# A list scheduler whose memory model is told 270 instead of 360 bytes per nanosecond

## The chip, the cores and the metric

The kernel runs on one core of a Trainium2 chip. That core has five engines that work side by side, each through its own list of instructions in a fixed order: TensorE (PE: matrix products, with a part that loads weights, PEld), VectorE (DVE), ScalarE (ACT), GpSimd (POOL) and SyncE (SP), which here does nothing but issue transfers. They meet at semaphores. The metric is the device time of one execution in microseconds (us).

## The reference

Three layers run one after the other on 4 x 576 = 2304 tokens of width 512, all in float32:

```python
# attention: 4 batches, 8 heads, 576 positions, head width 64
scores = scale * np.matmul(q, k.transpose(0, 1, 3, 2))
kth = np.partition(scores, -32, axis=-1)[..., -32:-31]
scores = np.where(scores >= kth, scores, -1000000000.0)
attn = softmax(scores); x = attn @ v
# a small MLP, 512 -> 2048 -> 512 (its weights arrive as float64)
h = x @ w_in
x = (h * np.cos(h)) @ w_out
# eight experts, 512 -> 1024 -> 512, every token through all of them
P = exp(x @ w_gate - max), normalised 8 times by rows and by columns
out = sum(P[:, e] * (np.maximum(x @ w1[e], 0) @ w2[e]) for e in range(8))
```

## The kernel before

Nothing is issued while the program is written down. Every step is put into a plan (`add`, through `put` and `dma`) with its engine, an estimate of its duration in nanoseconds, what it reads and writes, and a priority. At the end `Plan.issue` runs a list scheduler over the plan: it keeps a clock for each engine, takes the engine that can go on first, and there the ready step of the best priority (class of work first, then program order). The order in which it does so is the order in which each engine's instructions are emitted. The chip then runs these lists as they are: an engine whose next instruction waits does not take another one first. So the planner's estimates change no instruction; they change the order.

A step on one engine becomes ready for another after the latency in the table `LAT`. A transfer is a step on SP with a cost of its own; then the planner lets it pass through one shared queue (`dma_free`) at a fixed number of bytes per nanosecond, and its data are ready 900 ns later. The clock of TensorE is modelled as well (the cost doubles when it was not busy enough).

The work, in the order of the time line:

- *Leading tiles.* The first 3 tiles of 128 tokens (tile 0, 1, 2) go alone through attention (`attention_tile`) and the small MLP (`moe1_tile_a`, `moe1_tile_b`) in plain float32, so that expert work for them can begin early. A head's attention: score matmul (L451), copy to SBUF (L457), then on VectorE the search for the 32nd largest of 576 scores: four MAX8 (L459, L465) and three MATCH_REPLACE8 (L464), then the masked exponential (L466) and a reciprocal (L469); GpSimd scales (L468, L470), TensorE transposes (L475) and multiplies with v (L530), ScalarE copies the result into the tile's `x_f` (L534). The MLP multiplies with w_in (L631), forms the gate (L590 to L597), transposes (L640), multiplies with w_out (L656), transposes back (L663) and forms the logits of the gate network (L604, L605). Its weights come through four buffers `wp` of 512 KB.
- *Decode.* Beside that the float64 weights of the small MLP are turned into float32 by DVE, ACT and POOL (L325 to L333) and written back to memory (`win_d`, `wout_d`), from where `wp` reads them.
- *Attention of batch 0 onwards* (`attention`) with the score as a product of split operands (L447, L448) and the product with v at L501 and L503. Its key buffers (`kh`, `kl`, `qs`, made at L345, L347, L430, L431) lie in memory that the decode used before, so it starts after the last decode step.
- *Expert work for the 3 leading tiles* (`fill`, matmuls at L372 to L374): it fills TensorE while VectorE is busy with attention. Its buffers lie where the leading tiles' buffers were, so it starts when all three leading tiles are done.
- The small MLP of the next 512 tokens (`moe1`, 690 to 800 us; L372 to L374, L383, L384, L387), more attention with more expert work for 4 tiles, the MLP for the rest, and from about 1600 us on the experts for the other 15 tiles on TensorE.

TensorE multiplies float32 operands in two ways here: plain (L451, L530, L631, L656: two records in the trace for each matmul) and as products of a high and a low part.

## Time and profile before

| | |
|---|---|
| median of 3 runs | 2468.45 us (2467.83 to 2468.59) |
| the profiled execution | 2470.82 us, span 2469.0 us |
| mean granted TensorE clock | 0.981 |
| busy: TensorE, VectorE, ScalarE, GpSimd | 2367.0, 1988.3, 1279.0, 1282.3 us |
| moved by transfers | 267.44 MB |

The span runs from the first to the last instruction of the profiled execution; what is left of its 2470.82 us lies around it. Times in the rows below count from the span's start. A chain of waits leads back from the last instruction; 58% of it lies on TensorE and 21% on VectorE.

### The profile page before, as it was taken

The page shows a single profiled execution, that of the slowest core. Times are in us where ns is not written, and L with a number is a line of the kernel's source. Part 1 is how long each engine was busy: PE and PEld are TensorE (multiplying, and loading weights), DVE is VectorE, ACT ScalarE, POOL GpSimd, SP SyncE. Part 2 cuts the span into 40 slices and gives each one's busy share as a digit, 9 for nine tenths or more (in the row PEclk, how much of TensorE's full clock was granted, in tenths as well). Part 3 has the DMA queues.
Part 4 walks back from the last instruction along what each step waited for, and adds up shares of the span by engine and source line. Part 5 has one row for each costly group of instructions (what it writes and reads, how often), then busy time and mean ns, then how long its engine had stood idle before and what let it go on. Part 6 is the DMA issues. An engine that isn't in the chain of part 4 may idle for free.

```text
span 2469.0 us, 33830 instructions
## 1 busy us (share of the span) xinstructions
PE 2367.0 (96%) x11161; PEld 1906.4 (77%) x11161; DVE 1988.3 (81%) x3659; ACT 1279.0 (52%) x2470; POOL 1282.3 (52%) x1352
## 2 busy tenths in 40 slices
PE   6888899999988999999999999999999999999999
PEld 3444588888866887888887888788888888888887
DVE  8998599999999999999987787776666666666655
ACT  6785566666787666666666675323222222222221
POOL 6886487778886566666520034433433334443330
PEclk9679999999999999999999999999999999999999
DMA  8766654545522333343343333022222221111101
GB/s 266 225 211 197 192 167 143 159 131 175 172 77 86 115 116 116 119 119 100 91 122 116 97 111 96 26 65 89 78 84 79 73 60 35 39 43 39 35 22 48
DMA packets 162449, 267.44 MB, mean 108 GB/s; under 512 B 15392, under 2 KB 62576, under 8 KB 162272
## 3 DMA queue, kind: packets, MB, share of 16 engines
q1 hardware_dynamic: 162272, 265.27, 35.7%
q8 instruction: 88, 1.44, 0.3%
q14 instruction: 89, 0.73, 0.1%
HBM read 233.34 MB, written 31.87 MB: 107 GB/s over the span
## 4 chain that ended last, share of the span: by engine, by line
PE 58%; DVE 21%; POOL 4%; issue 3%; ACT 2%; DMA 1%; POOLq 0%; SPq 0%; ACTq 0%; DVEq 0%
PE y L372 9%; PE y L373 9%; PE y L374 9%; DVE wk L464 5%; DVE m L465 4%; DVE ex L466 3%; PE g L374 2%; PE g L373 2%; PE g L372 2%; DVE atl L494 1%; PE y L383 1%; PE y L387 1%; DVE m L459 1%; PE y L384 1%; DVE gl L761 1%
## 5 line engine op out<-in xcount | busy, mean ns | idle before, releaser
L347 POOL TENSOR_TENSOR wlo<-raw,whi 128x512 fp32r<-128x512 f32 x336 | 455.8, 1360 | 192.2 <-ACT whi L345 104.1
L465 DVE MAX8 m<-wk 128x8 f32<-128x576 f32 x432 | 318.1, 748 | 1.8
L955 DVE SCALAR_TENSOR_TENSOR acc<-y,P,acc 128x512 f32<-128x512 f32 x308 | 228.7, 747 | 99.6 <-PE y L374 99.3
L345 ACT ACTIVATE whi<-raw 128x512 fp32r<-128x512 f32 x416 | 259.3, 627 | 92.5 <-PE y L374 32.1
L464 DVE MATCH_REPLACE8 wk<-m,wk 128x576 f32<-128x576 f32 x288 | 213.6, 742 | 1.6
L372 PE MATMUL y<-whi,gh 128*128 128x512 f32 x448 | 181.6, 405 | 0.0
L372 PE MATMUL y<-gh,xh 128*128 128x512 f32 x450 | 177.2, 394 | 0.0
L373 PE MATMUL y<-gl,xh 128*128 128x512 f32 x450 | 176.4, 392 | 0.0
L374 PE MATMUL y<-whi,gl 128*128 128x512 f32 x448 | 176.3, 393 | 0.0
L374 PE MATMUL y<-gh,xl 128*128 128x512 f32 x450 | 176.1, 391 | 0.0
L373 PE MATMUL y<-wlo,gh 128*128 128x512 f32 x448 | 175.8, 392 | 0.0
L475 PE MATMUL t<-ident,ex 128*128 128x128 f32 (+1 forms) x720 | 135.6, 288 | 31.3 <-POOL ex L470 6.2
L457 ACT ACTIVATE sc<-s 128x288 f32<-128x288 f32 x288 | 117.2, 407 | 88.8 <-DVE ex L466 46.0
L475 PEld LDWEIGHTS t<-ident,ex 128*128 128x128 f32 (+1 forms) x720 | 86.5, 140 | 94.4 <-POOL ex L470 22.9
L466 DVE SCALAR_TENSOR_TENSOR ex<-sc,m,ex 128x576 f32<-128x576 f32 x144 | 154.6, 1074 | 1.6
L461 ACT ACTIVATE ex<-sc,m 128x576 f32<-128x576 f32 x144 | 111.4, 774 | 38.7 <-POOL m L460 37.2
L470 POOL TENSOR_SCALAR ex<-ex,m 128x576 f32<-128x576 f32 x144 | 112.5, 782 | 33.0 <-DVE m L469 30.4
L493 ACT ACTIVATE ath<-t 64x128 fp32r<-64x128 f32 (+3 forms) x272 | 104.6, 396 | 47.9 <-PE t L475 46.1
L459 DVE MAX8 m<-sc 128x8 f32<-128x576 f32 x144 | 107.0, 744 | 10.0 <-ACT sc L457 9.9
L464 DVE MATCH_REPLACE8 wk<-m,sc 128x576 f32<-128x576 f32 x144 | 106.6, 740 | 0.1
L372 PEld LDWEIGHTS y<-gh,xh 128*128 128x128 f32 x450 | 85.2, 189 | 19.0 <-DVE acc L951 1.0
L372 PE MATMUL y<-gh,gh 128*128 128x512 f32 x254 | 99.4, 391 | 0.0
(376 smaller groups left out, 7093.9 us busy)
## 6 DMA issues: line engine op xcount, KB each, us to landing
raw<-in_w_dram SPq DMA_DIRECT2D x384, 256.0 KB, 2.7
kq<-in_kq_dram SPq DMA_DIRECT2D x40, 576.0 KB, 4.2
raw<-win_d SPq DMA_DIRECT2D x64, 256.0 KB, 3.0
raw<-wout_d SPq DMA_DIRECT2D x64, 256.0 KB, 2.6
y_d<-st SPq DMA_DIRECT2D x56, 256.0 KB, 3.3
raw<-y_d SPq DMA_DIRECT2D x56, 256.0 KB, 2.7
wp<-win_d SPq DMA_DIRECT2D x24, 512.0 KB, 4.8
wp<-wout_d SPq DMA_DIRECT2D x24, 512.0 KB, 4.3
```

The costliest lines, as they stand in the source:

```text
L345: put("ACT", act_ns(n), lambda: A_.activation(hv(), rv(), AF.Copy), [rb], [hb])
L347: put(e, c, lambda: f.tensor_tensor(lv(), rv(), hv().bitcast(F32), op=ALU.subtract), [rb, hb], [lb])
L372: T_.matmul(o(), ah(), bh(), start=start, stop=False)
L373: T_.matmul(o(), ah(), bl(), start=False, stop=False)
L374: T_.matmul(o(), al(), bh(), start=False, stop=stop)
L457: put("ACT", act_ns(288, psum=True), lambda c=c: A_.activation(sc.ap[:, c], o(), AF.Copy), [ps_s], [(sc, c.start, c.stop)])
L459: put("DVE", 669, lambda: V.max(mc(0, 8), sc.ap), [sc], [(m, 0, 8)])
L464: put("DVE", 669, lambda r=r, src=src: V.match_replace(wk.ap, mc(8 * r, 8), src.ap, LOWEST), [src, (m, 8 * r, 8 * r + 8)], [wk])
L465: put("DVE", 669, lambda r=r: V.max(mc(8 * r + 8, 8), wk.ap), [wk], [(m, 8 * r + 8, 8 * r + 16)])
L466: put("DVE", 729, lambda: V.scalar_tensor_tensor(ex.ap, sc.ap, mc(31), ex.ap, op0=ALU.is_ge, op1=ALU.mult, accum_out=mc(33)), [sc, ex, (m, ...
L475: T_.transpose(pt()[:p, c - c0, :], ex.ap[:, c * 128 : c * 128 + p], ident.ap)
L955: put("DVE", 663, lambda y=y, av=av, pcol=pcol: V.scalar_tensor_tensor(av(), y.ap, pcol(), av(), op0=ALU.mult, op1=ALU.add), [y, P, a], [a])
```

## The change

The planner's rate for transfers falls from 360 to 270 bytes per nanosecond. This is the whole diff:

```diff
@@ -197,7 +197,7 @@
                     a = z
             free[e] = op.end = t + cost
             if e == "SP":
-                dma_free = max(t + cost + 650.0, dma_free) + op.bytes / 360.0
+                dma_free = max(t + cost + 650.0, dma_free) + op.bytes / 270.0
                 op.end = dma_free + 900.0
             order.append(k)
             for o in op.outs:
```

Both programs have the same instructions on every engine. Three places show how their order moves. The numbers at the ends of names are buffer numbers, which differ between the two programs.

TensorE at the end of tile 2's attention, in the program of before: from the last L530 of that tile on. `h` and `y` are accumulators, `x_f_277` is tile 2's input to the MLP, `gT` is a gated tile, and L656 with `gT_1242` belongs to tile 1.

```order
L530 MATMUL t<-at_f_304,vp_101 64x128 x5
L447 MATMUL s<-kh_1383,qt_1372 128x288
L448 MATMUL s<-kl_1388,qt_1372 128x288
L447 MATMUL s<-kh_1399,qt_1380 128x288
L448 MATMUL s<-kl_1419,qt_1380 128x288
L631 MATMUL h<-wp_366,x_f_277 128x512
L631 MATMUL y_353<-wp_512,x_f_277 128x512
L631 MATMUL h<-wp_322,x_f_277 128x512 x2
L631 MATMUL y_353<-wp_446,x_f_277 128x512 x2
L631 MATMUL h<-wp_366,x_f_277 128x512 x2
L631 MATMUL y_353<-wp_512,x_f_277 128x512 x2
L656 MATMUL y_1232<-wp_322,gT_1242 128x512 x2
```

The same engine and place in the program of after, from the same L530 on; `gT_814` is the gated tile 0, `x_f_257` tile 2's input.

```order
L530 MATMUL t<-at_f_282,vp_101 64x128 x5
L656 MATMUL y_1246<-wp_368,gT_814 128x512 x2
L656 MATMUL y_1246<-wp_404,gT_814 128x512 x2
L656 MATMUL y_1246<-wp_493,gT_814 128x512 x2
L631 MATMUL h<-wp_368,x_f_257 128x512 x2
L447 MATMUL s<-kh_1427,qs_1435 128x288
L448 MATMUL s<-kl_1437,qs_1435 128x288
L631 MATMUL h<-wp_404,x_f_257 128x512 x2
L447 MATMUL s<-kh_1427,qs_1435 128x288
L448 MATMUL s<-kl_1437,qs_1435 128x288
L656 MATMUL y_1246<-wp_577,gT_814 128x512 x2
L447 MATMUL s<-kh_1442,qs_1445 128x288
```

Tile 0's last eight matmuls at L656 and six of tile 2's at L631, as well as the first score matmuls of the next attention, stood ahead of that L530 and now stand behind it. Counted from it to the first L372, there are 10 of L631 and 32 of L656 before, and 16 and 40 after.

ScalarE at the same time, before: `kh`, `qs`, `qt` and `vs` are the next attention's prepared operands, `x_f_277` is filled by tile 2; the last L534 that fills it stands 28 rows behind the first `kh`.

```order
L461 ACTIVATE ex_223<-sc_213,m_267 128x576
L345 ACTIVATE kh_1383<-kq_117 128x576
L430 ACTIVATE qs_1386<-kq_117 128x128
L430 ACTIVATE qt_1372<-kq_117 128x64
L534 ACTIVATE x_f_277<-t 64x128
L345 ACTIVATE vs_1393<-vraw_120 128x5x64
L345 ACTIVATE kh_1399<-kq_122 128x576
L479 ACTIVATE at_f_304<-t 128x512
```

ScalarE after, where the first L534 shown is tile 2's last:

```order
L479 ACTIVATE at_f_282<-t 64x128
L534 ACTIVATE x_f_257<-t 64x128
L345 ACTIVATE kh_1427<-kq_115 128x576
L430 ACTIVATE qs_1435<-kq_115 128x128
L430 ACTIVATE qt_1429<-kq_115 128x64
L345 ACTIVATE vs_1440<-vraw_119 128x5x64
L345 ACTIVATE kh_1442<-kq_122 128x576
L430 ACTIVATE qs_1445<-kq_122 128x128
```

The preparation stood among tile 2's copies and now stands behind the last of them.

TensorE in the small MLP of the next 512 tokens, before: L383 and L384 multiply a gated tile `gh` with w_out, L447 and L448 here are the second half of one head tile's score matmul.

```order
L383 MATMUL y_353<-gh_2057,whi_1726 128x512
L384 MATMUL y_353<-gh_2057,wlo_1741 128x512
L447 MATMUL s<-kh_1399,qs_1406 128x288
L448 MATMUL s<-kl_1419,qs_1406 128x288
L383 MATMUL y_766<-gh_2057,whi_1726 128x512
L384 MATMUL y_766<-gh_2057,wlo_1741 128x512
```

The same half tile after, where `h<-xh` is the first product of that MLP:

```order
L373 MATMUL h<-xl,whi_1795 128x512
L374 MATMUL h<-xh,wlo_1803 128x512
L447 MATMUL s<-kh_1442,qs_1445 128x288
L448 MATMUL s<-kl_1456,qs_1445 128x288
L475 MATMUL t<-ident,ex_222 64x128
L372 MATMUL h<-xh,whi_1795 128x512
```

It moved forward over some 130 rows of that MLP.

## Rows read from the trace of the kernel before

**Rows 1.** The page, part 1: busy time, share of the span, instructions.

```profile
PE 2367.0 (96%) x11161; PEld 1906.4 (77%) x11161; DVE 1988.3 (81%) x3659; ACT 1279.0 (52%) x2470; POOL 1282.3 (52%) x1352
```

**Rows 2.** Busy time by stretches; clock, transfer share and GB/s last.

```profile
10.10:229.00 218.90, 180.19 (x561) 88.82 (x562) 208.00 (x392) 161.62 (x306) 176.01 (x183) 0.81 0.73 229
...
231.10:289.50 58.40, 52.73 (x195) 27.42 (x195) 28.17 (x55) 25.67 (x50) 18.18 (x24) 0.99 0.64 207
...
690.00:800.00 110.00, 92.07 (x434) 71.61 (x433) 103.52 (x167) 85.33 (x140) 82.41 (x74) 1.00 0.28 83
800.00:1283.00 483.00, 481.00 (x2431) 393.65 (x2430) 467.92 (x1022) 299.41 (x631) 280.43 (x353) 1.00 0.38 113
...
238.10:289.50 51.40, 45.73 (x153) 23.05 (x153) 21.28 (x41) 21.98 (x40) 16.88 (x20) 0.98 0.67 221
196.00:238.10 42.10, 35.90 (x156) 19.69 (x156) 37.07 (x76) 24.92 (x53) 28.24 (x35) 0.96 0.59 188
```

**Rows 3.** VectorE's waits, 10.1 to 229 us: total, times, longest.

```profile
DVE m L469 <- POOL m L468: 3.0, 2, 1.7
DVE d_mag L325 <- POOL d_low L333: 2.1, 2, 1.3
DVE d_sgn L331 <- POOL d_mag L330: 2.0, 3, 0.9
...
DVE d_mag L325 <- DMA d_raw<-in_w_in_dram: 0.6, 1, 0.6
```

**Rows 4.** TensorE's longest wait, 238.1 to 289.5 us.

```profile
PE y L656 <- DMA wp<-wout_d: 1.9, 1, 1.9
```

**Rows 5.** Time line of TensorE: start, duration, instruction, idle time before it.

```profile
236.72 1.45 PE L530 MATMUL t<-at_f,vp 128*64 128x128 f32 x10
...
289.51 0.52 PE L372 MATMUL g<-x2fh,whi 128*128 128x384 f32 x1
```

**Rows 6.** TensorE's costliest group, 238.1 to 289.5 us: busy us, mean ns.

```profile
L656 PE MATMUL y<-wp,gT 128*128 128x512 f32 x64 | 28.8, 595 | 1.9 <-DMA wp<-wout_d 1.9
```

**Rows 7.** Time line of TensorE: transposes, then one score matmul to the next start.

```profile
221.59 0.63 PE L475 MATMUL t<-ident,ex 128*128 128x128 f32 x4 [0.45 <-ACT x_f L534]
223.01 0.40 PE L447 MATMUL s<-kh,qs 128*128 128x288 f32 x1 [0.79 <-POOL qs L431]
...
223.38 0.27 PE L475 MATMUL t<-ident,ex 128*64 128x128 f32 x1
```

**Rows 8.** Time line of TensorE: one attention product, from its start to the next.

```profile
293.69 0.35 PE L501 MATMUL t<-ath,vs 128*128 128x192 f32 x1 [0.81 <-DVE ath L494]
...
294.78 0.32 PE L447 MATMUL s<-kh,qt 128*128 128x288 f32 x1
```

**Rows 9.** Time lines of ScalarE and VectorE at the end of tile 2's attention.

```profile
220.21 0.67 ACT L345 ACTIVATE kh<-kq 128x576 fp32r<-128x576 f32 x1
...
228.92 0.16 DVE L469 RECIPROCAL m<-m 128x1 f32<-128x1 f32 x1 [1.33 <-POOL m L468]
...
231.15 0.75 DVE L459 MAX8 m<-sc 128x8 f32<-128x576 f32 x1
```

**Rows 10.** TensorE's four longest waits in total, 690 to 800 us.

```profile
PE t L475 <- DVE atl L494: 4.4, 4, 1.5
PE t L475 <- DVE ath L494: 4.1, 3, 2.5
PE t L501 <- DVE ath L494: 4.0, 2, 2.6
PE s L447 <- ACT sc L457: 3.4, 1, 3.4
```

**Rows 11.** Busy time by stretches, the first two of 50 us.

```profile
0.00:50.00 50.00, 30.05 (x75) 14.58 (x75) 39.46 (x82) 33.05 (x63) 29.17 (x38) 1.00 0.91 290
50.00:100.00 50.00, 43.05 (x120) 20.58 (x121) 49.59 (x97) 35.94 (x73) 41.29 (x43) 0.66 0.72 222
```

**Rows 12.** One line's instructions, 88 to 104 us: duration in ns, least/median/most.

```profile
L631 PE MATMUL y<-wp,x_f x6: 1057/1061/1221, 91.9 to 102.2; 128*128 128x512 f32 x6
```

## Prediction

> **What bounds the kernel now.** I read the page first, then the busy time by stretches, then what VectorE and TensorE waited for, then a few short stretches instruction by instruction. The page shows TensorE busy for 96% of the span and VectorE for 81% [rows 1]. By stretches [rows 2] the reader is to see that they do not bind in the same place. Until 229 us VectorE is the full one: from 10.1 to 229 us it is busy 208.0 of 218.9 us, while TensorE, though busy for 180 us, runs at a mean granted clock of 0.81. From 231.1 to 289.5 us VectorE has work for 28.2 of 58.4 us and TensorE for 52.7. From 289.5 us on TensorE is nearly full (481 of 483 us between 800 and 1283 us), but for one long stretch, 690 to 800 us, where it is busy 92.1 of 110. So after 289.5 us the time is the sum of TensorE's work and of its few gaps, and what a new order can change is when that moment comes, and those gaps.
>
> Transfers are hardly waited for: VectorE waits 0.6 us for one in its full stretch [rows 3], TensorE 1.9 us in the stretch before 289.5 us [rows 4].
>
> **What the change does.** One number in the planner: a 512 KB load holds the modelled queue 524288/270 = 1942 ns where it held 524288/360 = 1456. No instruction is added, removed or made longer; each engine has the same ones in another order. From some 1500 us on the orders are nearly the same on every engine, so a cost must lie before that. I went through them for the places where TensorE waits or is waited for, and found two that matter.
>
> *Place one, the end of the leading tiles.* Tile 2's last attention product (L530) ends on TensorE at 238.1 us, and the first expert matmul (L372), which may only start when the third tile's small MLP is done, starts at 289.5 us [rows 5]. Between the two the order of before has 10 matmuls at L631 and 32 at L656; the order of after has 16 and 40. With transfers thought slow, the plan puts tile 0's last matmuls and tile 2's first ones, which use such loads, behind tile 2's attention, and leaves a hole ahead of it in which TensorE has little to do. Step by step:
>
> 1. 14 more plain matmuls. Each is two records; L656 shows 64 records in 28.8 us, 0.45 us each [rows 6], so 14 x 0.90 = 12.6 us.
> 2. Tile 0's closing transposes (a set of four takes 0.6 us, [rows 7]) and its eight small logit records (taken as another 0.5 us, an estimate from the same row) move behind tile 2 as well: 1.1 us.
> 3. Four score matmuls of the next attention that stood ahead of that L530 now stand behind it; one takes from 223.01 to the next start at 223.38 us [rows 7]: 4 x 0.37 = 1.5 us.
> 4. Five pieces of that attention that stood behind the first expert matmul now stand ahead of it: two products at L501/L503 of 1.1 us each [rows 8], a set of transposes of 0.6, a last transpose and a score matmul of 0.4 together: 3.2 us. TensorE has to do these anyway; they delay the expert work but are not lost.
>
> Lost in the queue is 12.6 + 1.1 + 1.5 = 15.2 us. Against it stand the gaps: between 238.1 and 289.5 us TensorE was busy 45.7 of 51.4 us [rows 2], so 5.7 were idle. A longer queue can fill these or keep them, since each is a short wait on another engine: I take half, -2.9.
>
> VectorE's side of the same place: ScalarE made the next attention's keys (kh, L345) at 220.2 us, under tile 2, and VectorE's first scan of it (L459) came at 231.2 us, right behind tile 2's last reciprocal at 228.9 [rows 9]. In the new order ScalarE has kh behind the last x_f copy of tile 2, so that scan can come only some 14 us later: the product ends at 238.1, then a copy, eight preparation pieces (kh, one of the longest, is 0.67 us), a score and its copy. TensorE does not wait for VectorE there as long as VectorE's work fits under TensorE's: four head tiles of eight passes of 0.75 us make 24 us, the MLP and the splits some 10, together 34 in a stretch of about 65. So I cost it at nothing; without that cover TensorE would wait before the transposes that now stand ahead of the expert work, on top of the 15.2.
>
> When does tile 2's attention end? VectorE, the full engine there, has the same work ahead of that end in both orders. The preparation that GpSimd did under tile 2 leaves, and VectorE's waits for L468 (3.0 us, [rows 3]) were partly behind it; the last decode pieces stand there instead. Between 0 and -3.0 us I take -1.5. The bounds are wider: all of VectorE's 10.9 idle us could go, or as many come.
>
> *Place two, 690 to 800 us.* TensorE has 17.9 us of gaps there [rows 2], most of them waits in front of attention pieces that its order has too early for VectorE or ScalarE [rows 10]. The longest, 3.4 us, is the second half of a head tile's score matmul, which waited for the ScalarE copy that frees the score bank. In the new order it stands some 31 us of TensorE work earlier, soon behind its first half, and so does that copy. I take this gap as gone: -3.4. The other attention pieces move by 2 to 8 us towards earlier, and VectorE's by about as much; I cost that at nothing, between -12.5 (the other three rows of waits go) and +5 (they grow by some 40%).
>
> Sum: 15.2 - 2.9 - 1.5 - 3.4 = 7.4 us; with something for the late VectorE I take **+8 us**. The profiled execution took 2470.8 us, 2.4 above the median of the three runs, 2468.45; it would take 2479, and the median is forecast at 2476.4.
>
> *Does the trace ask for 270?* The highest rate over a 50 us stretch is 290 GB/s, with the transfer engines 0.91 busy [rows 11]. So 270 is 7% below what the transfers did when they were fullest, and a plan made with it postpones work that could have started; that takes nothing from the sum. [...]
>
> **Rivals.** *No change.* Tile 2's attention could end some 7 us earlier, because VectorE's waits for GpSimd (L468, L330, L333: 7.1 us, [rows 3]) go when decode and attention are mixed otherwise. For it: the new order has decode later and tile 2's first scans earlier. Against it: GpSimd is busy 176 of the 218.9 us and keeps the same pieces. That gives 8 - 7 = 1, so 2469.5.
>
> *Faster.* One mechanism: in place two the attention on VectorE runs further ahead of TensorE, since 46 of its attention instructions now stand between tile 2's last reciprocal and the third tile's last split where 30 stood. If the four rows of waits there go (15.9 us, [rows 10]) and not one alone, the sum is 15.2 - 2.9 - 1.5 - 15.9 = -5.1, so 2463. It decides as soon as more than 10.8 us are given back. Against it: the order within that stretch is nearly the same, so I expect most of these waits again.
>
> [...]
>
> That the change does nothing is no rival, since the order differs on every engine.
>
> **How the numbers follow.** A measurement of this kernel tells some 0.2%, 4.9 us, from no change. Forecast as above: 0.55, with 2470 to 2485 as its own range (gaps all filled or all kept, tile 2 up to three us earlier or later, place two between -3.4 and +2). No change: 0.22. Faster: 0.12. Slower by the clock: 0.11. With about 0.2 left out, half of the faster case and the far ends of the others, the range is 2463 to 2489. Slower by over 0.2% is most of the forecast and the clock's case, 0.62; within 0.2% the no-change case and the forecast's low end, 0.26; faster 0.12.
>
> **What would show it.** The first L372 of the expert work at 300 to 308 us instead of 289.5; 112 records of L631 and L656 between tile 2's last L530 and it, instead of 84; TensorE well under 36 of 42 us busy just ahead of that L530; VectorE idle for some 14 us behind tile 2's last L469. Between 690 and 800 us no wait of 3.4 us on a score copy. From 800 us on, every stage as long as before. I am wrong if that L530 ends more than 5 us earlier, if the first L372 stays near 290, or if the stages behind 800 us change by more than 3 us in sum, since I cost them at nothing.

## Result and the profile after

| | median, us | lowest to highest | runs |
|---|---|---|---|
| before | 2468.59 | 2467.83 to 2473.37 | 5 |
| changed | 2497.08 | 2493.63 to 2499.49 | 5 |

The ratio is 1.0114, with an interval of 1.0103 to 1.0126: slower by 28.5 us. The forecast was +8 and a range that ended at 2489. The profiled execution has a span of 2495.3 us, 26.3 more than before. The page of the changed kernel, part 1 (its columns as in [rows 1]):

```profile
PE 2379.7 (95%) x11161; PEld 1913.8 (77%) x11161; DVE 1994.1 (80%) x3659; ACT 1284.6 (51%) x2470; POOL 1285.8 (52%) x1352
```

Same counts, and only 12.7 us more of TensorE's busy time: at least half of those 26.3 us is TensorE standing still. Where? The time line of TensorE in the changed kernel, at four places (start, duration, instruction, idle time before it and what ended it):

```profile
229.33 1.45 PE L530 MATMUL t<-at_f,vp 128*64 128x128 f32 x10
...
305.60 0.39 PE L372 MATMUL g<-x2fh,whi 128*128 128x384 f32 x1
...
1308.15 0.31 PE L501 MATMUL t<-ath,vs 128*128 128x320 f32 x1
1312.28 0.79 PE L383 MATMUL y<-gh,ch 128*128 128x512 f32 x1 [3.82 <-ACT ch L345]
```

The first L372 comes at 305.60 us, 16.1 later than in [rows 5]: place one went as forecast. The last line is a wait that I had not looked at, in the second part's MLP.

For the rest I paired each TensorE instruction of the two traces and read how much later TensorE has the same amount of work behind it (work counted by the durations of before, at a given time of before). This lateness is worked out from many rows; work that is only done in another order does not show in it.

| time in before, us | 300 | 800 | 1250 | 1300 | 1600 |
|---|---|---|---|---|---|
| changed kernel is late by, us | 12.8 | 9.8 | 17.7 | 26.6 | 25.7 |

Up to 800 us the change costs 9.8 us, about what I forecast. The step that failed is the last one of the forecast: "From 800 us on, every stage as long as before". There 7.9 us are lost slowly between 800 and 1250 us, and 8.9 at once between 1250 and 1300.

Busy time by stretches in the changed kernel (columns as in [rows 2]):

```profile
188.00:230.00 42.00, 31.66 (x115) 16.78 (x114) 33.09 (x58) 27.73 (x46) 34.29 (x32) 0.80 0.41 131
230.00:306.00 76.00, 67.05 (x233) 33.80 (x232) 36.34 (x73) 33.74 (x70) 24.27 (x36) 0.96 0.64 215
...
200.00:210.00 10.00, 8.80 (x27) 4.94 (x26) 10.00 (x21) 6.38 (x12) 5.77 (x7) 0.53 0.34 105
...
250.00:260.00 10.00, 9.12 (x15) 3.49 (x15) 6.49 (x16) 1.73 (x4) 2.60 (x7) 0.66 0.26 73
...
800.00:1250.00 450.00, 442.43 (x2231) 359.70 (x2232) 442.66 (x953) 281.14 (x590) 269.46 (x341) 1.00 0.37 109
...
1309.00:1330.00 21.00, 17.72 (x64) 14.02 (x65) 7.30 (x11) 6.09 (x10) 0.00 (x0) 0.84 0.28 81
```

And the long stretch of before, which [rows 2] have only with a later end:

```profile
800.00:1250.00 450.00, 448.00 (x2274) 366.21 (x2273) 443.00 (x977) 279.00 (x594) 276.92 (x348) 1.00 0.38 111
```

Between 800 and 1250 us both engines are nearly full in both kernels. VectorE is even busy for the same time, 443 us, but with 953 instructions for 977: the same work takes it longer. TensorE got 2231 matmuls done where it had done 2274.

**Why VectorE takes longer.** VectorE's groups between 800 and 1310 us in the changed kernel; of those with more than 20 instructions, the only one whose mean moved by more than 3 ns (busy us, mean ns):

```profile
L466 DVE SCALAR_TENSOR_TENSOR ex<-sc,m,ex 128x576 f32<-128x576 f32 x61 | 67.3, 1103 | 0.6
```

and in before:

```profile
L466 DVE SCALAR_TENSOR_TENSOR ex<-sc,m,ex 128x576 f32<-128x576 f32 x60 | 56.8, 946 | 0.7
```

L466 masks the scores, once a head tile, and reads two tensors from SBUF, the core's on-chip memory (`sc` and `ex`). Undisturbed it takes 0.80 us (0.80 to 0.83 in the 30 cases of the changed kernel that are not stretched), so 60 of them should take 48: I call what is above that its stretching, 56.8 - 48 = 8.8 us before and 67.3 - 48.8 = 18.5 after. One of the stretched ones, on VectorE:

```profile
960.18 1.68 DVE L466 SCALAR_TENSOR_TENSOR ex<-sc,m,ex 128x576 f32<-128x576 f32 x1
```

and what GpSimd did meanwhile, the low half of an expert weight block:

```profile
959.95 1.29 POOL L347 TENSOR_TENSOR wlo<-raw,whi 128x512 fp32r<-128x512 f32 x1 [1.09 <-ACT whi L345]
```

GpSimd's instruction ends at 961.24, L466 at 961.86, 0.62 us later. 31 of the 61 took over 0.85 us in this stretch, and all of them end 0.61 to 0.62 us behind one of GpSimd's subtractions L347, which read SBUF too; for 25 of them it is the low half of an expert weight block. In before 24 of 60 took that long. The neighbours with one wide input from SBUF, L464 and L465, take 0.73 to 0.76 us in this stretch of both kernels, whatever GpSimd does. The trace has the other case too: eight times in the changed kernel the low half of an expert weight block starts 0.06 to 0.55 us behind an L466. There L466 takes 0.80 to 0.82 us, and GpSimd's instruction 1.42 to 1.90 for the usual 1.3. So of two that met like this, the one that started second took longer.

**What happens at 1308 us.** TensorE's waits in the changed kernel, from 1277 to 1387 us (total, times, longest):

```profile
PE y L383 <- ACT ch L345: 3.8, 1, 3.8
PE y L383 <- ACT gh L345: 1.6, 1, 1.6
PE t L475 <- POOL ex L470: 0.6, 1, 0.6
PE t L501 <- DVE x L509: 0.4, 1, 0.4
```

In before, between 1260 and 1360 us, there is the wait for `gh` (1.3 us) and 0.3 for another; none for `ch`. `ch` and `cl` are the sixth pair of weight buffers of the second part's MLP, and the kernel takes them from the pool `ph2`, which opens only when all of attention is through. ScalarE's time line shows the end of that chain:

```profile
1308.50 0.43 ACT L508 ACTIVATE avt<-t 64x320 f32<-64x320 f32 x1 [0.78 <-PE t L501]
1311.60 0.63 ACT L345 ACTIVATE ch<-raw 128x512 fp32r<-128x512 f32 x1 [2.67 <-DMA x_d<-x]
```

Last product, copy, sum, the transfer of attention's last result, and only then the first write to `ch`. The chain is the same before. But there TensorE's order has 12 steps of that MLP ahead of attention's last product and 23 between it and the first that needs `ch`; attention's last record and that first one, in before:

```profile
1271.94 0.31 PE L501 MATMUL t<-ath,vs 128*128 128x320 f32 x1
...
1288.33 0.40 PE L383 MATMUL y<-gh,ch 128*128 128x512 f32 x1
```

Those 23 steps last from 1272.1 to 1288.3 us, and the wait lies under them. The new order has 36 ahead and none between. The 3.8 us stand bare, and TensorE's clock falls behind them: 0.84 in the mean from 1309 to 1330 us, as the stretch above shows, with 0.50 first and 1.00 after it (columns as in [rows 2]):

```profile
1312.28:1318.69 6.41, 6.41 (x14) 4.75 (x15) 1.36 (x2) 1.21 (x2) 0.00 (x0) 0.50 0.18 48
1318.69:1330.00 11.31, 11.31 (x51) 9.27 (x50) 5.46 (x8) 4.25 (x8) 0.00 (x0) 1.00 0.39 117
```

The 14 matmuls at 0.50 take 6.4 us, the next 14 take 3.2. So of the 8.9 us some 3.8 are the wait and 3.2 the clock behind it.

### The profile page after: what moved, and what is told of

Same layout as the page of the kernel before. It is cut to its first block, busy times and chain, and to the rows that moved or that the text cites. A ratio compares the mean times of both kernels' runs of the same rounds, so it can differ in the third digit from the quotient of the medians.

```text
span 2495.3 us, 33801 instructions
## 1 busy us (share of the span) xinstructions
PE 2379.7 (95%) x11161; PEld 1913.8 (77%) x11161; DVE 1994.1 (80%) x3659; ACT 1284.6 (51%) x2470; POOL 1285.8 (52%) x1352
## 4 chain that ended last, share of the span: by engine, by line
PE 44%; DVE 10%; ACT 2%; issue 1%; POOL 1%; DMA 0%; ACTq 0%; POOLq 0%
PE y L372 7%; PE y L373 7%; PE y L374 7%; DVE wk L464 2%; DVE m L465 2%; PE y L383 1%; PE y L384 1%; PE y L387 1%; PE g L374 1%; PE g L373 1%; PE g L372 1%; DVE ex L466 1%; PE y L887 1%; PE y L888 1%; PE h L889 1%; PE h L887 1%
## 5 line engine op out<-in xcount | busy, mean ns | idle before, releaser
L347 POOL TENSOR_TENSOR wlo<-raw,whi 128x512 fp32r<-128x512 f32 x336 | 458.4, 1369 | 281.9 <-ACT whi L345 193.4
L465 DVE MAX8 m<-wk 128x8 f32<-128x576 f32 x432 | 318.2, 748 | 2.4
L464 DVE MATCH_REPLACE8 wk<-m,wk 128x576 f32<-128x576 f32 x288 | 213.7, 742 | 1.4
L372 PE MATMUL y<-whi,gh 128*128 128x512 f32 x448 | 182.5, 407 | 0.0
L372 PE MATMUL y<-gh,xh 128*128 128x512 f32 x450 | 176.5, 392 | 0.7 <-DVE acc L951 0.7
L475 PE MATMUL t<-ident,ex 128*128 128x128 f32 (+1 forms) x720 | 135.9, 289 | 42.5 <-POOL ex L470 22.1
L466 DVE SCALAR_TENSOR_TENSOR ex<-sc,m,ex 128x576 f32<-128x576 f32 x144 | 169.1, 1175 | 1.7
L475 PEld LDWEIGHTS t<-ident,ex 128*128 128x128 f32 (+1 forms) x720 | 86.7, 140 | 106.2 <-POOL ex L470 36.9
L461 ACT ACTIVATE ex<-sc,m 128x576 f32<-128x576 f32 x144 | 111.6, 775 | 47.3 <-POOL m L460 46.1
L470 POOL TENSOR_SCALAR ex<-ex,m 128x576 f32<-128x576 f32 x144 | 110.6, 768 | 36.9 <-DVE m L469 36.4
L464 DVE MATCH_REPLACE8 wk<-m,sc 128x576 f32<-128x576 f32 x144 | 106.6, 741 | 0.0
L374 PEld LDWEIGHTS y<-whi,gl 128*128 128x128 f32 x448 | 84.1, 188 | 20.5 <-DVE gl L761 1.5
L372 PEld LDWEIGHTS y<-gh,xh 128*128 128x128 f32 x450 | 84.9, 189 | 19.3 <-DVE acc L951 1.3
```

What stands on the lines that cost most here:

```text
L347: put(e, c, lambda: f.tensor_tensor(lv(), rv(), hv().bitcast(F32), op=ALU.subtract), [rb, hb], [lb])
L372: T_.matmul(o(), ah(), bh(), start=start, stop=False)
L374: T_.matmul(o(), al(), bh(), start=False, stop=stop)
L461: put("ACT", act_ns(S, ap=True), lambda: A_.activation(ex.ap, sc.ap, AF.Exp, scale=0.125, bias=mc(32)), [sc, (m, 32, 33)], [ex], func="exp")
L464: put("DVE", 669, lambda r=r, src=src: V.match_replace(wk.ap, mc(8 * r, 8), src.ap, LOWEST), [src, (m, 8 * r, 8 * r + 8)], [wk])
L465: put("DVE", 669, lambda r=r: V.max(mc(8 * r + 8, 8), wk.ap), [wk], [(m, 8 * r + 8, 8 * r + 16)])
```

## Experiments

Each expectation stood before its run. Lateness is that of the profiled run, at times of before; stretching is L466's between 800 and 1310 us. Before's own median was 2467.1 to 2469.4 us beside these runs, while its profiled execution, against which lateness is measured, took 1.4 to 3.7 us longer than that; so a lateness at the end lies some us below the difference of the medians. In e2, f4, g3, h3 and i1 the times scatter over 7 to 11 us; the profiled execution is the slowest of e2 and one of the faster of the others.

| run | median, us | ratio, interval | late at 300 | 800 | 1250 | 1300 | 1600 | stretching |
|---|---|---|---|---|---|---|---|---|
| before | 2468.6 | | 0 | 0 | 0 | 0 | 0 | 8.8 |
| changed | 2497.1 | 1.0103 to 1.0126 | 12.8 | 9.8 | 17.7 | 26.6 | 25.7 | 18.5 |
| e1_lead270 | 2478.8 | 1.0027 to 1.0056 | 0.9 | 0.2 | 7.3 | 7.3 | 8.1 | 14.1 |
| e2_rest270 | 2487.5 | 1.0061 to 1.0091 | -6.1 | -5.6 | 3.6 | 20.1 | 19.0 | 19.9 |
| e3_dve14 | 2483.8 | 1.0050 to 1.0080 | 14.4 | 12.1 | 12.6 | 12.6 | 11.5 | 8.8 |
| e4_pe14 | 2479.6 | 1.0029 to 1.0059 | 10.9 | 9.5 | 9.0 | 9.0 | 7.9 | 8.7 |
| f1_slim_before | 2460.0 | 0.9956 to 0.9979 | -1.5 | -3.8 | -8.3 | -8.3 | -8.4 | 3.4 |
| f2_slim_after | 2479.7 | 1.0028 to 1.0062 | 12.4 | 7.3 | 1.2 | 8.7 | 7.5 | 2.8 |
| f3_r315 | 2486.8 | 1.0056 to 1.0086 | -6.6 | -6.6 | 3.2 | 18.5 | 15.7 | 15.8 |
| f4_r425 | 2471.5 | 1.0009 to 1.0028 | -2.6 | -4.8 | -2.5 | 2.8 | 0.8 | 11.2 |
| g1_ring5_after | 2484.0 | 1.0048 to 1.0078 | 11.5 | 8.2 | 16.2 | 16.7 | 12.5 | 18.5 |
| g2_thin_after | 2493.6 | 1.0088 to 1.0118 | 10.7 | 8.1 | 16.0 | 23.2 | 22.2 | 18.5 |
| g3_turn | 2474.2 | 1.0018 to 1.0037 | -2.2 | -4.3 | 0.5 | 0.5 | -0.7 | 12.6 |
| g4_turn_after | 2493.8 | 1.0088 to 1.0118 | 11.9 | 8.9 | 15.1 | 23.2 | 22.1 | 17.2 |
| h1_pieces | 2478.6 | 1.0030 to 1.0060 | -0.7 | -3.1 | 5.6 | 6.6 | 6.3 | 8.5 |
| h2_pieces_all | 2482.0 | 1.0044 to 1.0074 | 4.2 | 9.3 | 11.1 | 11.8 | 9.7 | 7.8 |
| h3_pieces_ring5_after | 2491.9 | 1.0087 to 1.0121 | 7.5 | 4.6 | 17.8 | 19.3 | 13.9 | 8.0 |
| h4_pieces_ring5_rest | 2473.3 | 1.0015 to 1.0039 | -9.1 | -7.2 | 8.3 | 8.3 | 2.5 | 10.8 |
| i1_ring5_before | 2468.0 | 0.9980 to 1.0004 | -0.2 | -2.1 | -1.1 | -1.5 | -4.5 | 9.0 |
| i2_slim_ring5_after | 2469.2 | 0.9992 to 1.0010 | 15.2 | 11.1 | 4.6 | 4.7 | -1.1 | 2.9 |

### Which part of the plan costs: one stage at a time

The first four runs set two theories against each other. A: VectorE's late start at place one is never made up, and delays everything. B: place one costs what was forecast, and the rest comes from the order behind 800 us.

```diff
-    ... + op.bytes / 360.0
+    ... + op.bytes / (270.0 if op.prio[0] < 2 else 360.0)   # e1: leading tiles and decoding alone
+    ... + op.bytes / (360.0 if op.prio[0] < 2 else 270.0)   # e2: all the others
```

> 270 only for the transfers of the leading tiles and the decode, 360 for all others; every instruction of before. Its order has place one as after has it (the key preparation on ScalarE behind tile 2's last copy, 53 plain matmuls behind tile 2's last L530, 42 before, 56 after) and attention's end as before has it (7 steps of the next small MLP ahead of it on TensorE; 12 before, 36 after). Theory A (VectorE's lost time at place one is never given back, delays attention's end at about 1283 us and TensorE with it): 20 to 28 us slower than before. Theory B (place one costs the forecast 8 to 10 us and the rest comes from the order that 270 makes between 800 and 1360 us): 8 to 11 us slower.

> The other half: 360 for the leading tiles and the decode, 270 for all other transfers; every instruction of before. Place one as before has it (44 plain matmuls behind tile 2's last L530), attention's end as after has it (36 steps of the next small MLP ahead of it). Theory A: within 5 us of before. Theory B: 14 to 20 us slower than before.

The two halves cost 11.6 and 20.2 us, together 31.8 for 28.5. Most of the cost has nothing to do with place one: e2 is ahead of before by 5.6 us at 800 and late by 20.1 at 1300. A is out. But e1 is not "place one" either, as I took it at first: it is level with before at 800 us and loses its 7 us between 800 and 1250, with the rate of 360 there; its stretching is 14.1. That does not clear the order in that stretch: paired by line and tiles, 9% of TensorE's instructions there stand at the same place in its list as in before's (0.3% in the changed kernel's).

At place one e1 has nearly the changed kernel's queue, 106 records of L631 and L656 for 112. But tile 2's last L530 starts at 226.26 us there, 10.5 earlier than in [rows 5], and the first L372 at 294.56, 5.1 later: with tile 2's attention ending earlier, nearly the same queue costs 0.9 us at 300 us.

Where e2 loses its 16.5 us between 1250 and 1300, TensorE's waits from 1257 to 1382 us:

```profile
PE h L374 <- DVE wlo L347: 4.9, 1, 4.9
PE y L383 <- ACT ch L345: 3.8, 1, 3.8
PE y L383 <- ACT gh L345: 1.6, 1, 1.6
```

The same wait for `ch`, and one for VectorE ahead of it.

The other two keep before's order and lose time at place one, on VectorE or on TensorE: one instruction is issued 19 or 29 times.

```diff
+    again = {1218: 18}   # e3: the first scan L459 of the next attention; e4: {1095: 28}, transposes L640 of tile 2
     for k in order:
-        ops[k].emit()
+        for _ in range(1 + again.get(k, 0)):
+            ops[k].emit()
```

> The order of before, but VectorE does its first scan (L459) of the attention behind the leading tiles 19 times instead of once, with the same result: 18 x 0.75 = 13.5 us of VectorE's time at place one, and nothing else. Theory A: 10 to 18 us slower than before, with the loss showing at attention's end, near 1283 us. Theory B, and the prediction's costing of VectorE's late start at nothing: 0 to 4 us slower.

> The order of before, but TensorE does one set of tile 2's transposes (L640) 29 times instead of once, with the same result: about 28 x 0.46 = 13 us of TensorE's time between tile 2's last L530 and the expert work. Both theories: the first expert matmul 11 to 13 us later. Theory B: the end 10 to 13 us later, all lost, nothing added. Theory A: VectorE is held up by the part that waits for TensorE there, so 10 to 16 us.

e4: some 13 us lost by TensorE at place one cost 12.3, as both theories say. e3: the 19 scans take 15.07 us for 0.75, so 14.3 us lost by VectorE cost 16.6, where B said 0 to 4 and A 10 to 18. TensorE's longest wait there, 231 to 306 us, and the ScalarE instruction behind which it comes (L477 is before's L475, L613 its L611, L463 its L461):

```profile
PE t L477 <- ACT st L613: 14.0, 1, 14.0
...
244.28 0.77 ACT L463 ACTIVATE ex<-sc,m 128x576 f32<-128x576 f32 x1 [14.77 <-POOL m L462]
```

The transposes that wait are tile 2's own last ones. In before's order ScalarE has the next attention's exponential, which needs that scan, ahead of small copies on which these transposes wait; so the late scan holds up ScalarE, and tile 2's last L530 (L532 there) starts at 251.57 us and not at 236.72. VectorE has no slack in before's order. In the new one ScalarE has that attention's work behind tile 2's last copy, and VectorE stood idle for some 18 us at this place without holding up tile 2. Neither run touches the stretch behind 800 us: both keep before's order, its stretching (8.8 and 8.7) and, from 300 us on, a lateness that does not grow.

### Collisions: GpSimd's subtraction without its length

In both orders the subtraction L347 in fill's second pass is made over 8 of its 512 columns.

```diff
+    if slim and eng == "POOL":   # slim: while fill(e, LEAD, 4, two) is built
+        put(e, c, lambda: f.tensor_tensor(lv()[:, 0:8], rv()[:, 0:8], hv().bitcast(F32)[:, 0:8], op=ALU.subtract), [rb, hb], [lb])
+        return
     put(e, c, lambda: f.tensor_tensor(lv(), rv(), hv().bitcast(F32), op=ALU.subtract), [rb, hb], [lb])
```

> Order of before; from fill at 800 to 1260 us GpSimd's subtraction of each expert weight block (L347) is made over 8 of its 512 columns, so the low halves of these weights are not the reference's; its planned cost and so all orders stay. Theory C (collisions): in the traces so far VectorE's masking scan L466 is stretched wherever it meets such a subtraction and ends 0.61 us behind it; between 800 and 1310 us that is 8.8 us above 0.80 us a piece in before and 18.5 in the changed kernel. Without the subtractions L466 falls from a mean of 946 to below 860 ns here, but TensorE was busy 481 of 483 us, so the time stays: 2464 to 2469. Theory D (order: the loss behind 800 us is VectorE's 10 steps of the second part's MLP that now stand ahead of attention's end, and TensorE's waits in the new order): the same here, 2466 to 2469.

> The same edit in the order of the changed kernel (2497.1). Theory C: L466 falls from a mean of 1107 ns to below 860 between 800 and 1310 us, VectorE has some 15 us more, attention ends about 15 us earlier, and the 7.9 us between 800 and 1260 us and most of the 9.4 behind them come back: 2479 to 2485. Theory D: the order is the same, so the waits and the steps pulled ahead stay, and only little comes back: 2492 to 2497.

L466 falls to 846 ns in the changed order (L470 in this kernel):

```profile
L470 DVE SCALAR_TENSOR_TENSOR ex<-sc,m,ex 128x576 f32<-128x576 f32 x61 | 51.6, 846 | 0.6
```

and TensorE does more between 800 and 1250 us than in before, 2301 matmuls for 2274 (2231 in the changed kernel):

```profile
800.00:1250.00 450.00, 449.40 (x2301) 372.96 (x2300) 442.68 (x986) 289.08 (x607) 144.24 (x351) 1.00 0.37 111
```

17.4 us come back, as theory C said. Lateness falls by 6.1 between 800 and 1250 us where it rose by 7.9; in f1 by 4.5. With the collisions out, the new order costs nothing in that stretch. The edit also empties GpSimd's queue, a rival that it does not take apart from the collisions. It can be worth little: from 800 to 1250 us TensorE waits 3.1 us for GpSimd in the changed kernel (0.3 in before) and VectorE 1.0 us (1.1 in before). The step at 1250 to 1300 us stays (7.5), which C had given back too. f1 was expected to move nothing and gave 7.5 us: that TensorE was busy for 481 of 483 us [rows 2] did not mean that VectorE's time was free there.

### Other rates

```diff
-    ... + op.bytes / 270.0
+    ... + op.bytes / 315.0   # f3; f4: 425.0
```

> One number again: 315 bytes per ns. Its order has place one nearly as before (44 matmuls at L631/L656 behind tile 2's last product where before has 42 and the changed one 56), and as many steps of the second part's MLP ahead of attention's end as the changed one (36 on TensorE, 32 on VectorE). Theory C: no cost at place one; behind 800 us what the chance of the collisions gives, so the time over before is about L466's stretching over before's 8.8 us plus what attention's late end adds: 2468 to 2490, in step with that stretching. Theory D: the steps pulled ahead cost what they cost with 270 in that stretch alone (+20): 2480 to 2490, whatever L466 does. A third view, that a rate costs the more the lower it is: halfway, 2480 to 2485.

> 425 bytes per ns. Place one as before (42 matmuls); 30 steps on TensorE and 30 on VectorE of the second part's MLP ahead of attention's end (before 12 and 22). Theory C: again in step with L466's stretching, 2465 to 2485. Theory D: nearly as many steps pulled ahead as with 270, so +10 to +18: 2478 to 2487. The third view: a rate above 360 costs nothing: 2463 to 2469.

315 costs nothing up to 800 us, loses 9.8 to 1250 with a stretching of 15.8, and 15.3 at the step; 2486.8 is within what C and D gave, and does not tell them apart. 425, with 30 steps pulled ahead, should have cost 10 to 18 us by D and cost 4 (ratio 1.0018); its stretching is 11.2 and its loss to 1250 us 2.3. The view that a lower rate costs more has 315 nearly right, but 425 is no gain, and no view of the rate alone explains why e1 and e2 lose at different places.

### The step at 1300 us: gate or VectorE

```diff
-    whi_r.bufs, wlo_r.bufs = ring[0] + more[:1], ring[1] + more[1:]
+    whi_r.bufs, wlo_r.bufs = ring   # g1: five pairs, without ch and cl
```

> The changed kernel (2497.1), but the second part's MLP rotates its weights through five pairs of buffers instead of six; the sixth pair, ch/cl, lies in memory that attention gives back, and in the changed kernel TensorE waits 3.8 us for it from the end of the last attention product. The planner's order moves a little with it. Theory E (gate: the 9.4 us behind 1260 us are this wait, which the work pulled ahead no longer covers, and TensorE's slow start behind it): the 3.8 us wait on ch goes, and 5 to 7 us with it: 2490 to 2492. Theory V (VectorE's lateness sets the end of attention and so everything behind it): the lateness stays: 2495 to 2498.

```diff
     for k in order:
+        self.short = k in (7232, 7233, 7235, 7237, 7278, 7281, 7282, 7284, 7286, 7357)   # g2
         ops[k].emit()
...
+    if self.plan.short:      # around each call of nc.vector
+        a = [x[:, 0:8] for x in a]
```

> The changed kernel in its own order; the ten steps on VectorE of the second part's MLP that the new order has ahead of attention's last one (numbers 7232 to 7357 in the plan, 7.4 us by the durations of before) are made over 8 columns each, so those parts are not the reference's. Theory V: attention ends 7 us earlier and so does all behind it: 2489 to 2491. Theory E: TensorE is busy from 1277 to 1306 us with the steps pulled ahead in any case and then waits its 3.8 us: 2494 to 2498.

g1: the step falls from 8.9 to 0.5, and with it the wait. TensorE's waits there, 1276 to 1380 us:

```profile
PE y L383 <- ACT gh L345: 2.3, 1, 2.3
PE t L475 <- POOL ex L470: 0.8, 1, 0.8
```

g2 takes away 7.4 us of VectorE's work and keeps the wait of 3.82 us and a step of 7.2; 3.5 us come back, half of what V said, and its trace was ahead of the changed kernel's by 2.1 us at 300 us already, where the edit cannot act (the granted clock from 50 to 100 us was 1.00 there and 0.80 in the changed kernel). Gate, not VectorE, for the changed kernel. g1 gave back 13.0 us, more than the 5 to 7 expected: between 1500 and 1600 us its lateness falls from 19.3 to 12.5, where the changed kernel's falls from 27.2 to 25.7.

The control puts five pairs into before, where there is no wait to remove.

> Rate 360, and five pairs of weight buffers in the second part's MLP instead of six. Theory E: there is no wait at the gate to take away, so up to 1360 us nothing moves; what the five pairs gave at 1500 to 1550 us in the other runs has nothing to do with the rate and shows here too: 2461 to 2464. If all 13 us were the gate's: 2466 to 2469, or slower by a few us since a pair is missing.

Up to 1300 us it moves by 2 us at most, and from 1500 to 1600 us its lateness falls from 0.8 to -4.5, by as much as in g1. So of g1's 13 us some 8 are the gate's and some 5 a gain of the smaller ring that has nothing to do with the rate; why it comes there I did not follow up. In the median i1 is level with before (0.9980 to 1.0004), 4 us short of its expectation, so this gain stands in the traces and not in the times.

### Trying to avoid the collisions with nothing left out

```diff
+    if e == "POOL" and turns <= 0:   # g3 (rate 360), g4 (rate 270)
+        free_now = [x for x in now[e] if ops[x[1]].tag != "split" or ops[x[1]].ready < t - 9000.0]
+        if not free_now:
+            free[e] = t + 300.0
+            continue
...
+    if op.tag == "turn":      # L468
+        turns = 3
+    elif op.tag == "split":   # fill's L347
+        turns -= 1
```

> Rate 360 as in before; in the planner GpSimd's subtractions of fill's second pass get their turn only behind the small operation L468 (three at most, or after 9 us of waiting). L468 itself waits for VectorE's L466, so on the chip they run while VectorE does its other scans, and nothing is left out. The orders of the other engines stay nearly as in before. Theory C (collisions): L466's stretching between 800 and 1310 us falls from 8.8 us to below 5, and up to the 7.5 us come back that the shortened subtractions gave: 2460 to 2466. If the subtractions come too late for TensorE instead, its waits on them grow: 2470 or more. Theory D (order): nothing moves, 2466 to 2469.

> The same rule with the rate of 270. Theory C: L466's stretching falls from 18.5 us to below 8, and 6 to 14 of the 17.4 us come back that the shortened subtractions gave: 2483 to 2491. Theory D: 2494 to 2498.

Both failed: stretching rose to 12.6 in the order of before and fell only to 17.2 in the other. The rule shifts the subtractions in the model's time; on the chip L347 still has to wait for ScalarE's half of the split (`whi`): in before, between 800 and 1260 us, 61.1 us of GpSimd's idle time ended on it. That this undid the rule in g3 and g4 is my reading. g3 lost 4.8 us between 800 and 1250 us, in step with its stretching.

```diff
+    if parts and eng == "POOL":   # parts, in h1, h3, h4: fill's second pass; h2: all wide ones and the decoding, in two
+        def emit():
+            for p in range(4):
+                q = slice(p * n // 4, (p + 1) * n // 4)
+                f.tensor_tensor(lv()[:, q], rv()[:, q], hv().bitcast(F32)[:, q], op=ALU.subtract)
...
     put(e, c, lambda: f.tensor_tensor(lv(), rv(), hv().bitcast(F32), op=ALU.subtract), [rb, hb], [lb])
```

> Order and rate of before; each of GpSimd's subtractions of fill's second pass is made as four of 128 columns instead of one of 512, so that VectorE's L466, which waits for the piece under way, waits for a quarter of the time at most. Nothing is left out. Theory C (collisions): L466's stretching between 800 and 1310 us falls from 8.8 us to below 5, and 3 to 7 us come back: 2461 to 2465. If GpSimd's own time grows so that TensorE waits for the low halves: 2468 or more. Theory D (order): 2466 to 2469.

> Order and rate of before; every one of GpSimd's wide subtractions, and the three products and sums of the decoding, as two halves each. L466 was stretched by 39 us in all up to 1310 us in before, 10 of them before 300 us where VectorE is the full engine. Theory C: about half of the stretching goes; some 5 us at the leading tiles and some 4 behind 800 us come back, and what goes between 300 and 800 us lies under TensorE: 2457 to 2464. If GpSimd, busy 176 of 219 us in the leading stretch, becomes the bound there: 2470 or more.

Both are slower, by 11 and 15 us. In h2 GpSimd is busy for 202 of the 218.9 us up to 229 us, where it had 176 [rows 2], and VectorE waits 12.9 us for its decode pieces, where it had 4.1 [rows 3]. That goes the way of the second half of the expectation, but the lateness is 4.2 us at 300 us and 9.3 at 800, so less than half of the loss lies there. GpSimd's groups from 800 to 1260 us in h1:

```profile
L351 POOL TENSOR_TENSOR wlo<-raw,whi 128x128 fp32r<-128x128 f32 x492 | 224.2, 488 | 74.5 <-ACT whi L345 36.7 <-issue 23.0 <-PE t L484 4.6
```

and in before:

```profile
L347 POOL TENSOR_TENSOR wlo<-raw,whi 128x512 fp32r<-128x512 f32 x123 | 162.3, 1320 | 93.0 <-ACT whi L345 61.1 <-issue 17.8 <-ACT ath L493 5.4
```

A quarter takes 0.49 us and not 0.33, and behind the longer queue the small operation L468 comes late. VectorE's longest waits from 800 to 1283 us in h1:

```profile
DVE m L478 <- POOL m L477: 7.9, 17, 1.2
```

In before this wait was 1.4 us. The stretching did not fall (8.5), but not because the pieces hold VectorE as long as the whole did. One L466 (L475 in this kernel), the piece under way at its start and the next piece:

```profile
1219.15 0.99 DVE L475 SCALAR_TENSOR_TENSOR ex<-sc,m,ex 128x576 f32<-128x576 f32 x1
...
1219.05 0.47 POOL L351 TENSOR_TENSOR wlo<-raw,whi 128x128 fp32r<-128x128 f32 x1
...
1219.47 0.98 POOL L351 TENSOR_TENSOR wlo<-raw,whi 128x128 fp32r<-128x128 f32 x1
```

L466 ends 0.62 us behind the first piece, and the second takes twice its time: now GpSimd waits for VectorE. 12 of the 16 L466 that meet pieces get in between two of them like this, and the next piece takes 0.97 to 0.98 us each time, for 0.46 in the median. The longest L466 that met a piece is 1.10 us, for 1.60 with a whole subtraction in before, and these 16 are stretched by 2.9 us, for 4.9 with 14 in before. What they save is lost on the GpSimd instructions that were not cut, with which the stretching rises from 3.6 to 5.2 us, and on the longer queue.

> Rate 270, five pairs of weight buffers as in the first of the runs on the gate (2484.0), and fill's second-pass subtractions in four pieces. Theories C and E together: 5 to 11 us below 2484, 2473 to 2479; what is left over before is place one and two, +8 to +11. Theory D (the order has a cost of its own behind 800 us): 2482 to 2485.

> The same two edits with the rate of 270 for all but the leading tiles and the decoding (2487.5 without them). Place one is then that of before or better (in that run TensorE was 6 us ahead at 300 us). Theories C and E: nothing is left of the cost: 2458 to 2468. Theory D: the order of the rate of 270 behind 800 us keeps a cost of its own, 2475 to 2488.

h3's stretching is 8.0, but it loses 13.2 us between 800 and 1250 all the same, as h1 does 8.7, and it is slower than g1: VectorE's wait for L468 there is 13.1 us (1.0 in the changed kernel). The pieces cost more than they save, and it decides nothing. h4 gives back 14 of e2's 20 us and has no step at 1300 us; but it still loses 15.5 us between 800 and 1250, more than h1, so that nothing is left of the cost is not shown by it.

### Both causes out

i2 is the changed kernel with the shortened subtractions of f2 and the five pairs of g1, without the pieces.

> Rate 270, five pairs, and GpSimd's fill subtractions over 8 of 512 columns, so that the low halves of these weights are not the reference's. Theories C and E: both causes are out; what remains against the shortened subtractions in the order of before (2460.0) is place one and two, +8 to +11, less the 5 us at 1500 us: 2463 to 2468. Theory D (a cost of the order itself behind 800 us): 2472 to 2480.

2469.2, level with before, and between the two forecasts: 1.2 us above that of C and E, 2.8 below that of D. The trace decides: lateness falls by 6.5 between 800 and 1250 us, where f1's falls by 4.5, and there is no step (0.1). Theory D, a cost of the order itself behind 800 us, is out. Against f1, the same edit on GpSimd in the order of before, the profiled spans are 2468.6 and 2461.0. The lateness at 800 us differs by 14.9 (11.1 and -3.8), of which 5.2 stood at 200 us already (3.9 and -1.3); the ring gives some 5 back.

## Why the prediction was wrong

**Place one** was right in its sum and not in its parts. The first L372 was to come at 300 to 308 us and came at 305.60. L631 and L656 have 112 records between tile 2's last L530 and it, as forecast, VectorE is idle for 18 us behind tile 2's last L469 but for 0.43 us of small copies (some 14 forecast), and TensorE is busy for 31.7 of the 42 us ahead of 230 (well under 36 forecast). But tile 2's last L530 starts at 229.33 and not near 235: 7.4 us earlier than in [rows 5], where I had taken 1.5 and named more than 5 as a sign that I was wrong. That was the premise of the rival of no change. It came true, and the stretch from it to the first L372 grew by 23.5 us instead of 15.5 (15.2 - 2.9 + 3.2): TensorE's work there by more than I had counted (67.1 of 76 us, against 45.7 of 51.4 in [rows 2]), and its gaps to 9.0 us, where I had half of 5.7 filled. The two errors cancel, so that the sum came out is luck; e1 shows what it hangs on, where nearly the same queue behind a still earlier end of tile 2's attention cost 0.9 us. Some 3.6 of the 16.1 us are given back by 350 us, as term 4 had it (3.2).

**The clock.** The forecast has "Slower by the clock" with 0.11, and no run shows what a lower clock behind tile 2 would add. In the changed kernel the 20 us right behind tile 2's last L530, between 230 and 250 us, had 1.00. The clock fell ahead of them and after them: 0.53 from 200 to 210 us and 0.66 from 250 to 260. In before the lowest of such stretches of 10 us from 190 to 290 us is 0.83. The traces do not tell how much of place one this is.

**Place two** was right in its direction, and in one of its four waits. TensorE's waits there in the changed kernel, 700 to 820 us, beside [rows 10]:

```profile
PE t L475 <- DVE atl L494: 5.8, 4, 2.7
PE t L475 <- DVE ath L494: 4.5, 3, 2.4
PE t L501 <- DVE ath L494: 2.6, 2, 2.0
PE s L447 <- ACT sc L457: 1.4, 1, 1.4
```

The wait of 3.4 us on a score copy is gone, another of 1.4 is there, and the four rows sum to 14.3 for 15.9. Lateness falls by 2.1 us from 690 to 800 us, where I took -3.4, and by 3.0 in all from 300 on.

**Behind 800 us** I costed the change at nothing: "every stage as long as before", since TensorE was full there and I had found only two places where it waits or is waited for. That is the failed step, and it is 16.8 us of lateness. Two mechanisms take its place, both measured by taking them away:

- 7.9 us between 800 and 1250 us: VectorE's L466 meets a GpSimd instruction 31 times instead of 24 and loses more each time (0.60 us for 0.37), so its stretching grows from 8.8 to 18.5 us. Without the subtraction's length the loss is gone (f2, i2). In the runs with whole subtractions the loss in that stretch goes with the stretching: -0.5 to 1.0 at 8.7 to 9.0, 2.3 at 11.2, 4.8 at 12.6, 7.1 at 14.1, 6.2 at 17.2, 7.9 to 8.0 at 18.5, 9.2 at 19.9; 315 lies above with 9.8 at 15.8. Between f2 and the changed kernel that is 14.0 us of TensorE for 15.7 of stretching, 0.9 for one. Why its meetings cost more in the new order is not shown. It is not place one's lateness: e1 has none at 800 us and loses 7.1, with 23 meetings at 0.61 us each. That any other order moves the two engines against each other is my reading; each of the seven other orders that ran with whole subtractions loses 2.3 us or more in that stretch.
- 8.9 us between 1250 and 1300 us: the wait of 3.8 us for `ch`, bare because the new order has done the covering work ahead of attention's end, a lower clock behind it, and some small waits ahead. With five pairs it is gone (g1, i2). In all runs with 30 or more of that MLP's steps ahead of attention's last product and six pairs it stands: 3.8 us, and 2.5 with the rate of 425, whose order leaves six steps between that product and `ch`. In e1, with 7 ahead, and before, with 12, it does not. In e2 and with 315 the step is larger, 16.5 and 15.3 us: more waits come to it, and the clock from 1290 to 1310 us is 0.76 and 0.66.

What I had written for place one, that an idle VectorE costs nothing while its work fits under TensorE's, fits what the changed kernel did there, though no run tests it in that order, and in before's order e3 shows the opposite. It was not true behind 800 us, where both engines are full: there each us that VectorE lost cost TensorE nearly one (0.9 above). I had read TensorE's 481 of 483 us [rows 2] as a sign that it alone binds, and did not set VectorE's 467.9 beside it.

What stays open: how the 16 us of place one divide between queue, clock and gaps; why L466 loses more to GpSimd in every other order; why five pairs give 5 us at 1500 us; and what the wait of 4.9 us for VectorE in e2 is made of.

## What to carry to other kernels

Where two engines are both nearly full, as TensorE (448 of 450 us) and VectorE (443) were here between 800 and 1250 us, do not cost a new order at nothing: look for instructions of one line whose mean differs between places or orders, as that of L466 did (946 and 1103 ns), since here this showed a contention that the planner's table does not have. A pool that opens only behind a stage was here a wait whose cover was the order (3.8 us bare, none in before); count the steps that stand between that stage's end and the first use of the pool, before and after. And I know no way to read such a contention off the order ahead of a run, so a range for a reordered kernel has to hold it: in the orders tried here it was worth 2.3 to 9.8 us against before.

## What the runs showed of the hardware

- A VectorE instruction with two inputs from SBUF (L466) waited for a GpSimd one (L347), for up to 1.1 us (1.91 in all), and ended 0.61 to 0.62 us after it, in all 31 stretched cases of the changed kernel. Shortening one line of these GpSimd instructions in before gave 7.5 us.
- Cutting GpSimd's instruction into four shortened that wait: in h1 VectorE got in between two pieces in 12 of 16 meetings, took 1.10 us at most for 1.60, and the next piece then waited for it (0.97 to 0.98 us for 0.46). But a quarter of the columns took 0.49 us in the mean for 1.32, and the kernel was slower by 11 us.
- Transfers moved 364 GB/s over 10 us in e1 (270 to 280 us), and 318 in the same stretch of before. I had taken 290, the highest over 50 us [rows 11], as what they do when fullest; so 270 is further below than I said.
